# Attention of the first batch with transposes on PE and float32 products, and division behind the product

## The chip, the cores and the metric

The kernel runs on one core of a Trainium2 chip. The metric is device time in microseconds, the median of three runs. The core has a matmul engine (TensorE, PE below; its weight loads are PEld), a vector engine (VectorE, DVE), an activation engine (ScalarE, ACT), GpSimd (POOL) and SyncE (SP), which here only issues DMAs. PE writes its results to PSUM, which has eight banks of 512 float32 columns.

## What is computed

Three stages follow each other: attention with normalised q and k (4 batches, 12 heads, 448 positions, 64 columns), a gated layer with a matrix over the positions (`moe1` in the kernel), and a residual MLP behind a layer norm (`moe2`). All is float32.

```python
rms = lambda x, g: x / sqrt(mean(x * x, -1) + 1e-6) * g
s = (rms(q, g_q) @ rms(k, g_k).T) / sqrt(64)
p = exp(s - max(s)); p = p / (sum(p) + 1e-9)
x = heads_to_columns(p @ v)                     # 4 x 448 x 768
h = relu(x @ w_in); u, w = h[:512], h[512:]     # split of the 1024 columns
x = (u * (w_spatial @ norm(w) + b_spatial)) @ w_out
out = x + relu((norm(x) * g_ln) @ w_ch1) @ w_ch2
```

## The kernel before

**Numbers.** A float32 matrix is held as two float16 matrices, a high part and what is left (hi and lo), and a product is three float16 matmul passes (hi hi, hi lo, lo hi). Much of the work on DVE and ACT makes these parts. ACT makes hi by a converting copy, DVE makes lo as `x * scale - hi`, in one instruction.

**Attention.** It goes by pairs of heads; pair `i` of 24 belongs to batch `i // 6`. `att_load` (L156) loads q, k and v of a pair: q with its positions laid out `(n p)`, in rows of 256 bytes, k as `(p n)`, v twice, once for each half of the partitions. `att_front` and `att_back` (L171, L191) normalise q and k, split them, and turn them with a DMA transpose into `hT`. `att_v` (L208) scales v on POOL (L214), splits it on ACT and POOL (L215, L216). `s_mm` (L223) makes the scores of a group of two blocks of 128 rows; block 3 lies across both heads and runs as two 64-row halves (L232), the others as whole matmuls (L236). `softmax1` (L240) takes the maximum (L246, L247) and the exponentials with their sums (L251). `softmax2` (L260) makes the scaled reciprocal of the sums (L265, L266), the high part of the probabilities (L271, ACT) and the low part (L274, DVE), into `p16`, and one DMA transpose per group turns `p16` into `pT` (L276). `av_mm` (L280) multiplies with v: eleven steps, for each head 384 columns and then 64 (L293), the two heads on the two halves of PE's columns, into the single bank `ps_o`. `av_out` (L297) splits the result into `xT` (L304, L305). `att_slot` (L313) puts these in program order; the product of pair `i - 1` stands in the slot of pair `i`.

**The stages.** Pairs 0 to 6 run beside `moe1_weights` (L430), which loads the weights as 64-bit floats, rebuilds float32 by integer operations on DVE (L386 to L388) and splits them. The pairs of the next batch run beside `moe1` of the batch before (L482). The last `moe1` runs beside the layer norms and the first products of `moe2` (L612), which then goes on alone to the end. PSUM before `moe2`: three banks `ps_m` for `moe1` and the small sums, one `ps_o`, two times two for the scores (`ps_s`).

**The order.** At the end `issue_order` (L875) replaces the program order of each engine by that of a list scheduler, `schedule` (L796). It uses the costs of `hold` (L702), in ns, for instance for DMAs:

```python
    if kind == "InstDmaTransposeAnt":
        return 490 + 0.83 * n, 1325, 0.875 * n
    if kind == "InstDMACopy":
        ...
        x = p * b / (180 if short else 360)
```

The last value is the time of the transfer itself. The priorities are disturbed and relaxed again as the list `SHAKES` (L666) says.

## Time and profile before

| | us |
|---|---|
| median of 3 runs (lowest, highest) | 1217.05 (1215.68, 1217.31) |
| the profiled execution | 1218.43 |
| its span, first to last instruction | 1216.6 |
| PE busy | 1053.8 (87%) |
| DVE busy | 925.8 (76%) |
| ACT busy | 594.5 (49%) |
| POOL busy | 246.6 (20%) |

Busy time is an average over stages that have different limits, so the stretches are read one by one: attention of the first batch with the moe1 weights (until about 190 us), attention of the other batches with moe1 (190 to 480), the last moe1 with the first of moe2 (480 to 570), moe2 (570 to the end). PE's busy time contains the modelled end of each matmul, so matmuls that stand apart look longer than they pace in a dense row. Several names of a tile are joined in a row (`pT<-p`), and a row's mean is that of one instruction.

### The profile page before, as it was taken

To read this page: it belongs to the slowest core of one execution; us is meant where nothing else is said; L and a number is where in the kernel's file an instruction comes from. 1 tells how busy PE (TensorE), PEld (TensorE's weight loads), DVE (VectorE), ACT (ScalarE), POOL (GpSimd) and SP (SyncE) were. 2 spreads that over 40 slices of the span, in tenths; PEclk is the share of its full clock that TensorE was granted. 3 is DMA by queue.
4 is the path that set the end of the run, shared out by engine and by line. 5 is a ranking of instruction groups with operands and counts; after the bars stand their busy time and mean duration, and the time that the engine had idled before them with its cause. 6 is when DMAs were issued, how large, how long until landed. Compare 5 with 4: busy or idle time off the path is not lost.

```text
span 1216.6 us, 17589 instructions
## 1 busy us (share of the span) xinstructions
PE 1053.8 (87%) x6444; PEld 552.3 (45%) x6444; DVE 925.8 (76%) x1992; ACT 594.5 (49%) x1122; POOL 246.6 (20%) x164
## 2 busy tenths in 40 slices
...
GB/s 192 257 221 252 213 206 198 193 192 208 203 200 203 186 180 153 244 163 210 246 117 27 27 79 104 1 105 38 68 34 71 79 26 104 1 52 1 1 52 130
DMA packets 289430, 159.28 MB, mean 131 GB/s; under 512 B 253568, under 2 KB 266944, under 8 KB 289344
## 3 DMA queue, kind: packets, MB, share of 16 engines
...
## 4 chain that ended last, share of the span: by engine, by line
PE 58%; DVE 22%; DMA 9%; issue 4%; ACT 3%; POOL 2%; SPq 1%; ACTq 0%; POOLq 0%; DVEq 0%
PE ps L627 27%; PE ps L646 26%; DVE p L274 6%; DVE nb L246 4%; DMA pT<-p 2%; DVE nb L247 1%; DMA xnT<-xn 1%; DVE raw L197 1%; POOL rs L184 1%; DMA vraw<-in_v_dram 1%; PE pso L564 1%; PE ps_s L236 1%; DVE sm L265 1%; PE psu L523 1%; PE ps_o L293 1%
## 5 line engine op out<-in xcount | busy, mean ns | idle before, releaser
L646 PE MATMUL ps<-xnT,wt 128*128 128x384 f16 (+1 forms) x1728 | 358.6, 354 | 5.7 <-DMA xnT<-xn 5.7
L627 PE MATMUL ps<-wt,h 128*128 128x384 f16 x2016 | 356.3, 326 | 0.0
L630 DVE SCALAR_TENSOR_TENSOR x<-ps,wio,x 128x384 f32<-128x384 f32 x336 | 198.8, 613 | 131.7 <-PE ps L627 130.9
L627 PEld LDWEIGHTS <-h 128*128 128x128 f16 x2016 | 196.6, 98 | 136.9 <-ACT h L650 0.7
L646 PEld LDWEIGHTS <-wt 128*128 128x128 f16 x1728 | 168.1, 98 | 157.0 <-DMA xnT<-xn 6.2
L649 ACT ACTIVATE hf<-ps 128x512 f32<-128x512 f32 (+1 forms) x96 | 51.2, 540 | 354.0 <-PE ps L646 345.3
L236 PE MATMUL ps_s<-hT 128*128 128x448 f16 x288 | 88.1, 417 | 112.6 <-ACT pexp L251 77.4
L274 DVE SCALAR_TENSOR_TENSOR p<-pexp,sm,p 128x448 f16<-128x448 f32 x168 | 133.4, 811 | 7.9 <-ACT p L271 7.8
L251 ACT ACTIVATE pexp<-ps_s,nb,cs 128x448 f32<-128x448 f32 x168 | 119.8, 716 | 32.9 <-DVE nb L247 16.7
L271 ACT ACTIVATE p<-pexp,sm 128x448 f16<-128x448 f32 x168 | 104.2, 660 | 23.6 <-DMA pT<-p 9.9
L293 PE MATMUL ps_o<-pT,v 128*64 128x64 f16 (+1 forms) x1056 | 87.3, 297 | 23.4 <-DVE xT L305 13.1
L651 DVE TENSOR_TENSOR h<-hf,h 128x512 f16<-128x512 f32 (+1 forms) x96 | 59.1, 619 | 62.4 <-ACT h L650 61.7
L236 PEld LDWEIGHTS <-hT 128*128 128x128 f16 x288 | 27.9, 105 | 157.8 <-issue 89.0
L246 DVE TENSOR_REDUCE nb<-ps_s 128x2 f32<-128x896 f32 x96 | 92.0, 960 | 4.0 <-PE ps_s L236 2.4
L293 PEld LDWEIGHTS <-v 128*64 128x64 f16 x1056 | 51.1, 122 | 67.4 <-issue 21.1
L502 PE MATMUL psv<-w_v,xT 128*128 128x512 f16 (+1 forms) x360 | 68.0, 346 | 4.8 <-DVE xT L305 2.6
L523 PE MATMUL psu<-xT,w_u 128*128 128x448 f16 x288 | 64.3, 359 | 0.0
L184 POOL TENSOR_TENSOR rs<-ss,mhalf 128x28 f32<-128x28 f32 (+1 forms) x12 | 57.9, 4827 | 26.9 <-DVE sm L265 9.7
L357 ACT ACTIVATE wt<-r_f 128x1536 bf16<-128x1536 f32 x24 | 35.4, 1475 | 50.9 <-PE ps L627 44.6
L200 POOL TENSOR_TENSOR qk<-raw,qk 128x896 f16<-128x896 f32 x23 | 47.9, 2084 | 53.6 <-ACT qk L199 45.7
L650 ACT ACTIVATE h<-hf 128x512 f16<-128x512 f32 (+1 forms) x96 | 54.5, 575 | 5.4 <-PE ps L627 3.0
L387 DVE SCALAR_TENSOR_TENSOR r_f<-r_w,r_f 128x256 int32<-128x256 int32 (+1 forms) x96 | 53.5, 560 | 1.1
...
## 6 DMA issues: line engine op xcount, KB each, us to landing
...
```

Source lines behind the costliest of these rows:

```text
L184: nc.gpsimd.tensor_tensor(rs, ss, c.mhalf[:, 0:14 * m], op=ALU.pow)
L236: nc.tensor.matmul(ps[:, :S], p.hT[:, blk, :], kt[:, :, hd * 64:hd * 64 + 64], start=(t == 0), stop=(t == 1))
L246: nc.vector.tensor_reduce(nb[:, 0:n], ps[:, 0:n, :S], axis=AX.X, op=ALU.max, negate=True)
L251: nc.scalar.activation(pe[:, j, :], ps[:, j, :S], AF.Exp, bias=nb[:, j:j + 1], scale=c.cs[:, 0:1], accum_out=sm[:, j:j + 1])
L271: nc.scalar.activation(hi, x, AF.Copy, scale=sm[:, j:j + 1])
L274: nc.vector.scalar_tensor_tensor(lo, x, sm[:, j:j + 1], hi, op0=ALU.mult, op1=ALU.subtract)
L293: nc.tensor.matmul(p.po[hd * 64:hd * 64 + 64, c0:c1], p.v16[:, hd, u], p.pT[:, blk:blk + nb, ch, r0:r1], start=(n == 0), stop=(n == len(mm ...
L502: nc.tensor.matmul(ps[m * h:m * h + m, 0:hn], xT[:, k, x, t * P:t * P + m], wv[:, w, k, h * hn:(h + 1) * hn], start=(n == 0), stop=(n == l ...
L523: nc.tensor.matmul(ps[:, :S], wu[:, w, k, f * P:(f + 1) * P], xT[:, k, x, :], start=(n == 0), stop=(n == len(mms) - 1))
L627: nc.tensor.matmul(ps[:, 0:384], h16[:, f, h, t * P:(t + 1) * P], w2[:, w, f, e * 384:(e + 1) * 384], start=(i == 0), stop=(i == len(mms) ...
L630: nc.vector.scalar_tensor_tensor(xs, ps[:, 0:384], io[:, 0:1], xs, op0=ALU.mult, op1=ALU.add)
L646: nc.tensor.matmul(ps[:, 0:nn], w1[:, w, d, f * P:(f + 1) * P], xnT[:, a:a + n, x * NC6 + d, :], start=(i == 0), stop=(i == len(mms) - 1))
```

## The change

For the pairs of the first batch (0 to 5, `PE_PAIRS`) the exponentials stay float32. PE transposes them against an identity matrix, 28 blocks of 128 x 128 per pair (the last of four column blocks overlaps the third), into PSUM (`ps_t`, two banks), ACT copies them to `pT`, and PE multiplies them with the unsplit v in float32, four column blocks for each of two heads. These pairs have no `att_v`, no `p16`, no low part, no DMA transpose of `p16`, and no third load of v.

For all pairs the probabilities are no longer divided by their sum before they are turned. A new `av_scale` makes the reciprocals of seven sums, spreads them as a diagonal (`dg`, DVE), turns them into a row for each head with one float32 matmul into `ps_o`, and ACT copies that row to `rb`. `av_out` multiplies the product by it (DVE) and splits. The later pairs keep the float16 parts of the exponentials, two blocks in one instruction and without a scale from a tile.

q is loaded as `(p n)` like k, in runs of 1792 bytes. With it every block of rows holds positions of both heads, so all score blocks run in two halves, and the product runs with all 448 columns at once. Several tiles change their place (`gk`, `vpre`, `sq` with two buffers, the position weights loaded in two parts). PSUM has `ps_x` with one bank for the sums, `ps_t` with two until pair 6 is done, then `ps_m` with two; `moe2` gets five banks `ps_f` instead of four. The order model takes other DMA times, a cost of float32 matmuls, and a port that some DVE and POOL instructions share; `SHAKES` is another list.

```diff
 def att_load(c, i):
-    nc.sync.dma_start(out=r[:, 0:NB, :], in_=c.q[b, h0:h0 + 2].rearrange("h s d -> (h s) d").rearrange("(n p) d -> p n d", p=P))
+    nc.sync.dma_start(out=r[:, 0:NB, :], in_=c.q[b, h0:h0 + 2].rearrange("h s d -> (h s) d").rearrange("(p n) d -> p n d", p=P))
...
-    nc.sync.dma_start(out=vr[64:128, :, 6, :], in_=vs[:, :, 0, :])
+    if i not in PE_PAIRS:
+        nc.sync.dma_start(out=vr[64:128, :, 6, :], in_=vs[:, :, 0, :])
...
 def att_v(c, i):
+    if i in PE_PAIRS:
+        return
...
+CHUNKS = (0, 128, 256, S - 128)
+PE_PAIRS = {0, 1, 2, 3, 4, 5}
...
 def s_mm(c, i, g):
-            if blk == 3:
-                for hd in range(2):
...
-            else:
-                hd = int(blk > 3)
-                nc.tensor.matmul(ps[:, :S], p.hT[:, blk, :], kt[:, :, hd * 64:hd * 64 + 64],
-                                 start=(t == 0), stop=(t == 1))
+            for hd in range(2):
+                nc.tensor.matmul(ps[hd * 64:hd * 64 + 64, :S], p.hT[:, blk, hd * 64:hd * 64 + 64],
+                                 kt[:, :, hd * 64:hd * 64 + 64], start=(t == 0), stop=(t == 1))
...
 def softmax2(c, i, g):
-    nc.vector.tensor_scalar(sm[:, 0:n], sm[:, 0:n], 1e-9, 2.0 ** -14, op0=ALU.add, op1=ALU.mult)
-    nc.vector.reciprocal(sm[:, 0:n], sm[:, 0:n])
...
-            nc.scalar.activation(hi, x, AF.Copy, scale=sm[:, j:j + 1])
...
-        nc.vector.scalar_tensor_tensor(lo, x, sm[:, j:j + 1], hi, op0=ALU.mult, op1=ALU.subtract)
+    if i in PE_PAIRS:
+        for j, blk in enumerate(GROUPS[g]):
+            pt = c.ps_t.tile([P, 512], F32, tag="ps_t", name=f"ps_t{i}_{blk}")
+            for ch, k0 in enumerate(CHUNKS):
+                nc.tensor.transpose(pt[:, ch * P:(ch + 1) * P], p.pe[g][:, j, k0:k0 + P], c.ident[:])
+            nc.scalar.activation(p.pT[:, blk * 512:(blk + 1) * 512], pt, AF.Copy)
+        return
+    x = p.pe[g][:, 0:n]
+    p16 = c.att.tile([P, 2, 2, S], F16, tag="p16", name=f"p16_{i}_{g}", bufs=3)
+    nc.scalar.activation(p16[:, 0:n, 0], x, AF.Copy, scale=2.0 ** 14)
+    nc.vector.scalar_tensor_tensor(p16[:, 0:n, 1], x, 2.0 ** 14, p16[:, 0:n, 0], op0=ALU.mult, op1=ALU.subtract)
...
 def av_mm(c, i):
+    if i in PE_PAIRS:
+        pT = p.pT.rearrange("p (b c q) -> p b c q", b=NB, c=4)
+        for ch in range(4):
+            p0 = 64 if ch == 3 else 0
+            for hd in range(2):
+                nc.tensor.matmul(p.po[hd * 64:hd * 64 + 64, :S], p.vr[p0:, hd, 5 if ch == 3 else 2 * ch],
+                                 pT[p0:, :, ch, hd * 64:hd * 64 + 64], start=(ch == 0), stop=(ch == 3))
+        return
...
+    for n, (ch, u) in enumerate(mms):
+        for hd in range(2):
+            nc.tensor.matmul(p.po[hd * 64:hd * 64 + 64, :S], p.v16[:, hd, u], pT[:, :, ch, hd * 64:hd * 64 + 64],
+                             start=(n == 0), stop=(n == len(mms) - 1))
+
+
+def av_scale(c, i):
...
+    nc.vector.tensor_scalar(p.sm, p.sm, 1e-9, None, op0=ALU.add)
+    nc.vector.reciprocal(p.sm, p.sm)
+    dg = c.att.tile([P, 64, NB], F32, tag="dg", name=f"dg{i}", bufs=1)
+    nc.vector.tensor_tensor(dg, p.sm[:].unsqueeze(1).to_broadcast([P, 64, NB]),
+                            c.eye2[:].unsqueeze(2).to_broadcast([P, 64, NB]), op=ALU.mult)
+    pr = c.ps_o.tile([P, 512], F32, tag="ps_o", name=f"ps_r{i}")
+    nc.tensor.matmul(pr[:, :S], c.head, dg.rearrange("p q n -> p (q n)"), start=True, stop=True)
+    p.rb = c.att.tile([P, S], F32, tag="dg", name=f"rb{i}", bufs=1)
+    nc.scalar.activation(p.rb, pr[:, :S], AF.Copy, scale=2.0 ** 14 if i in PE_PAIRS else 1.0)
...
 def av_out(c, i):
-    nc.scalar.activation(xT[:, hp, 0, :], p.po[:, :S], AF.Copy, scale=2.0 ** -14)
-    nc.vector.scalar_tensor_tensor(xT[:, hp, 1, :], p.po[:, :S], 2.0 ** -14, xT[:, hp, 0, :], op0=ALU.mult, op1=ALU.subtract)
+    x = c.att.tile([P, S], F32, tag="xo", name=f"xo{i}", bufs=1)
+    nc.vector.tensor_tensor(x.rearrange("d (p n) -> d p n", n=NB), p.po[:, :S].rearrange("d (n p) -> d p n", n=NB),
+                            p.rb.rearrange("d (p n) -> d p n", n=NB), op=ALU.mult)
+    if i in PE_PAIRS:
+        split(c, x, xT[:, hp, 0, :], xT[:, hp, 1, :], c.sv[b][:, 0:1])
+    else:
+        nc.scalar.activation(xT[:, hp, 0, :], x, AF.Copy)
+        nc.vector.tensor_tensor(xT[:, hp, 1, :], x, xT[:, hp, 0, :], op=ALU.subtract)
...
 def hold(i, eng, kind):
-        return 490 + 0.83 * n, 1325, 0.875 * n
+        return 490 + 0.83 * n, 1325, 1.17 * n
...
-        x = p * b / (180 if short else 360)
+        x = p * b / (218 if short else 256)
...
     if eng == "PE":
+        if any(x.dtype == F32 for x in i.ins):
+            return n * 4 / 2.37 + 2 if n > P else 115, 0, 0
...
 def tile_attention_moe_moe2_kernel(...):
-    c.ps_m = c.ps_x = ps_m = pool("ps_m", "left", 3, space=PSUM)
+    c.ps_x = pool("ps_x", "left", 1, space=PSUM)
+    c.ps_t = pool("ps_t", "left", 2, space=PSUM)
...
+    c.ident = eye = c.wraw.tile([P, P], F32, tag="ident", name="ident", bufs=1)
+    make_identity(nc, eye[:])
+    c.eye2 = c.const.tile([P, 64], F32, name="eye2")
+    nc.vector.tensor_tensor(c.eye2, eye[:, 0:64], eye[:, 64:P], op=ALU.add)
+    c.head = c.const.tile([P, P], F32, name="head")
...
+    c.ps_t.release()
+    c.ps_m = ps_m = pool("ps_m", "left", 2, space=PSUM)
...
-    c.ps_f = pool("ps_f", "right", 4, space=PSUM)
+    c.ps_f = pool("ps_f", "right", 5, space=PSUM)
```

## Rows read from the trace of the kernel before

**Rows 1.** Stretches: length, busy us per engine (instructions), granted clock, DMA share, GB/s.

```profile
core 0: us, PE busy (x) PEld busy (x) DVE busy (x) ACT busy (x) POOL busy (x), PEclk, DMA share, GB/s
0.00:30.00 30.00, 0.93 (x2) 0.13 (x2) 12.24 (x35) 5.31 (x6) 4.64 (x8) 1.00 0.89 191
30.00:190.00 160.00, 73.64 (x432) 30.68 (x432) 155.54 (x299) 121.52 (x240) 79.42 (x40) 0.85 1.02 228
190.00:360.00 170.00, 147.72 (x1073) 69.89 (x1071) 165.50 (x347) 143.80 (x295) 95.49 (x58) 0.96 1.04 199
360.00:480.00 120.00, 106.77 (x755) 50.85 (x757) 105.90 (x230) 92.04 (x188) 47.84 (x36) 0.93 0.92 181
...
570.00:1217.00 647.00, 641.58 (x3694) 359.94 (x3694) 413.23 (x891) 180.47 (x320) 0.00 (x0) 1.00 0.20 66
...
120.00:150.00 30.00, 14.23 (x76) 6.05 (x77) 30.00 (x63) 21.79 (x45) 13.42 (x8) 0.61 0.99 220
```

**Rows 2.** Chain of waits, shares by line, 30 to 190 us and 190 to 480.

```profile
by line: DVE p L274 15.0%; DVE nb L246 13.0%; issue 9.0%; DMA u_w<-in_moe_w_in_dram 5.4%; DVE raw L197 4.8%; DMA pT<-p 3.6%; DMA o_w<-in_moe_w_out_dram 3.4%; DVE nb L247 3.2%; DVE u_f L388 3.2%; POOL rs L184 3.0%; DVE o_f L387 2.9%; DVE sm 
...
by line: DVE p L274 15.6%; DVE nb L246 10.6%; issue 10.3%; DMA pT<-p 5.0%; PE psu L523 4.5%; PE ps_s L236 4.3%; DVE nb L247 4.1%; PE ps_o L293 3.9%; POOL rs L184 3.4%; DVE sm L265 3.1%; ACT pexp L251 2.9%; DVE raw L197 2.8%; ACT p L271 2.2%
```

**Rows 3.** Groups by line and form: DVE and POOL in attention and moe1.

```profile
L274 DVE SCALAR_TENSOR_TENSOR p<-pexp,sm,p 128x448 f16<-128x448 f32 x168 | 133.4, 811 | 7.9 <-ACT p L271 7.8
...
L265 DVE TENSOR_SCALAR sm<-sm 128x2 f32<-128x2 f32 x72 | 23.2, 325 | 1.1 <-ACT pexp L251 0.9
...
L265 DVE TENSOR_SCALAR sm<-sm 128x1 f32<-128x1 f32 x24 | 3.4, 140 | 0.0
...
L266 DVE RECIPROCAL sm<-sm 128x2 f32<-128x2 f32 x72 | 10.8, 152 | 0.2
...
L305 DVE SCALAR_TENSOR_TENSOR xT<-ps_o,xT 128x448 f16<-128x448 f32 x24 | 14.6, 609 | 3.1 <-ACT xT L304 3.1
...
L551 DVE SCALAR_TENSOR_TENSOR g<-u,wsc_g,g 128x448 f16<-128x448 f32 x16 | 9.9, 675 | 0.9 <-ACT g L550 0.9
...
L200 DVE TENSOR_TENSOR qk<-raw,qk 128x896 f16<-128x896 f32 x1 | 1.1, 1082 | 0.0
...
L216 POOL TENSOR_TENSOR v<-vraw,v 128x512 f16<-128x512 f32 x24 | 31.8, 1327 | 5.0 <-ACT v L215 5.0
```

**Rows 4.** Instructions on the tile sm: count, duration min/median/max ns, first and last start.

```profile
L274 DVE SCALAR_TENSOR_TENSOR p<-pexp,sm,p x168: 658/672/2309, 45.5 to 471.6; 128x448 f16<-128x448 f32 x168
```

**Rows 5.** Groups by line and form: ACT copies and conversions.

```profile
L271 ACT ACTIVATE p<-pexp,sm 128x448 f16<-128x448 f32 x168 | 104.2, 660 | 23.6 <-DMA pT<-p 9.9 <-DVE sm L266 7.0 <-issue 2.3
...
L199 ACT ACTIVATE qk<-raw 128x896 f16<-128x896 f32 x24 | 22.6, 943 | 17.1 <-DVE raw L197 13.9 <-DMA hT<-qk 3.2
...
L649 ACT ACTIVATE hf<-ps 128x512 f32<-128x512 f32 x48 | 28.0, 590 | 121.1 <-PE ps L646 116.2 <-DVE r_f L387 3.3 <-PE pssc L83 1.6
...
L550 ACT ACTIVATE g<-u,wsc_g 128x448 f16<-128x448 f32 x16 | 9.4, 655 | 4.7 <-DVE wsc_g L90 4.4 <-DVE wsc_g L89 0.3
```

**Rows 6.** Instructions on the tile pT: the transposes on SP's queue.

```profile
L276 SPq DMA_TRANSPOSE pT<-p x96: 1221/1645/4265, 46.8 to 472.3; - x96
```

**Rows 7.** Groups by line and form: PE and its weight loads.

```profile
L236 PE MATMUL ps_s<-hT 128*128 128x448 f16 x288 | 88.1, 417 | 112.6 <-ACT pexp L251 77.4 <-DMA hT<-qk 24.9 <-DMA hT<-hT 7.1
...
L293 PE MATMUL ps_o<-pT,v 128*64 128x384 f16 x528 | 74.9, 390 | 23.4 <-DVE xT L305 13.1 <-DMA pT<-p 6.1 <-POOL v L216 2.3
...
L523 PE MATMUL psu<-xT,w_u 128*128 128x448 f16 x288 | 64.3, 359 | 0.0
...
L236 PEld LDWEIGHTS <-hT 128*128 128x128 f16 x288 | 27.9, 105 | 157.8 <-issue 89.0 <-DMA hT<-qk 34.2 <-DMA hT<-hT 13.4
...
L293 PE MATMUL ps_o<-pT,v 128*64 128x64 f16 x528 | 19.5, 205 | 0.0
...
L232 PE MATMUL ps_s<-hT 128*64 128x448 f16 x96 | 17.5, 444 | 0.0
...
L83 PE MATMUL pssc<-ssb,ones 128*128 128x1 bf16 x24 | 4.0, 167 | 0.8 <-DVE ssb L80 0.8
```

99 lines of the change are left out of this document (52 added, 47 removed).

## The prediction

> **What bounds the kernel now.** First the stretches [rows 1]. From 570 us on PE is busy 641.6 of 647 us at full clock: moe2 is a wall of matmuls, which the change leaves as it is, apart from which PSUM pool its banks come from. Whatever can be won lies before. Between 30 and 190 us (attention of the first batch beside the conversion of the moe1 weights) DVE is busy 155.5 of 160 us and the DMA engines have work throughout (share 1.02), while PE has 73.6 us and ACT 121.5. Between 190 and 480 us (attention of the other batches beside moe1) DVE has 165.5 + 105.9 = 271.4 of 290 us, PE 147.7 + 106.8 = 254.5, ACT 235.8, DMA about full. So the first stretch is held by DVE and DMA with PE idle half the time; in the second, DVE and PE are close to each other. The chains of waits say the same [rows 2]: L274, the low half of the probabilities, is the largest piece of both, then L246; no PE line is named in the first stretch, and PE lines come in with 4 to 5% each in the second.
>
> **What each pair costs now and after, on DVE.** Removed per pair [rows 3]: seven L274 at 811 ns (5.68 us), L265 three times at 325 and once at 140 (1.12), four L266 at 152 (0.61), L305 (0.61): 8.01 us. Added for every pair by the division behind the product: an add over 7 columns (0.14 to 0.33, taken 0.25), a reciprocal (0.15), the diagonal `dg` with 448 columns (L551's form at 675, or L274's at 811: 0.74), the product out of PSUM (L305's 0.61), the low part (0.74 again): 2.49 us. A pair of the first batch has no low half of the exponentials left, so it saves 8.01 - 2.49 = 5.5 us, six pairs 33. A later pair keeps them, without a scale operand, three times with 896 columns (L200 on DVE has 1082 ns; stretched as L274 is, 1310; taken 1.2) and once with 448 (0.74): 4.34, so it saves 1.2 us, 18 pairs 21. The stretching is worth a look [rows 4]: L274 takes 672 ns at the median but up to 2309, so 168 x 139 ns = 23 us of its time is something holding it. First-batch pairs also lose L216 on POOL (1.3 us) and L214. If POOL is what holds DVE, up to 126 x 0.139 = 17 us more could go in the later pairs; I count none of it, and some in the low end.
>
> The Trainium skill (SBUF — State Buffer, on its shared port pair) says that a DVE instruction with two SBUF inputs contends with a GpSimd instruction that reads SBUF. The spread from 658 to 2309 ns agrees, and by that rule `dg` and the new low part are open to it too, which the 0.74 already covers.
>
> **ACT.** [rows 5] First batch, per pair: seven L271 (4.62), L215 (the form of L199: 0.94) and L304 go; seven copies of 512 columns out of PSUM (L649, 0.59 each: 4.13), the copy `rb` (the form of L304, which it replaces) and the high part with a scale (L550: 0.66) come. That is 0.8 us less, six pairs 5. Later pairs get three copies of 896 (0.94) and one of 448 (0.66) for seven of 0.66, `rb` for L304, and the high part: 0.5 us less. The new copies stand between two PE steps, which L271 did not.
>
> **DMA.** A first-batch pair drops the transposes of p16, 7 x 2 x 448 x 128 x 2 bytes = 1.6 MB; at the stretch's 228 GB/s [rows 1] that is 7.0 us, six pairs 42 of the 163 us (1.02 x 160) of work. Its third load of v (32 KB) goes too. In the queue they leave SP free: one L276 transpose holds SP's queue 1.6 us at the median and up to 4.3 [rows 6], and the loads of q, k, v and weights stand behind it. The load of q in contiguous runs of 1792 bytes, not 256, costs no more than before; its gain lies between 0 and its whole transfer (224 KB, 1.0 us a pair), counted 0.
>
> **PE, where the trace shows least.** No row has a float32 matmul or a transpose on PE, so both are bounded [rows 7]. A dense pass of 448 columns paces at 64.3 / 288 = 223 ns (L523), so 128 columns stream in 64 ns; a weight load takes 105 ns (L236) and overlaps PE.
> - 28 transposes per pair: low, stream alone, 28 x 64 ns = 1.8 us; high, four passes each with its load in the open, 28 x 4 x 169 ns = 18.9. Taken: the load sets the pace as loads overlap in every PE row here, 28 x 0.105 = 2.9.
> - Eight float32 products of 448 columns: low, one pass with the two halves of PE side by side as L293 runs now (four pairs of 0.33: 1.3 us); high, four passes each with a 105 ns load in the open, 8 x 4 x 328 = 10.5. Taken: four passes one behind the other, 8 x 4 x 223 = 7.1, since the new `hold` books four times the columns and no discount for the second half.
> - L293 in float16 goes: (74.9 + 19.5) / 24 = 3.9 us. The product for `rb` comes: 4 x 223 = 0.9 (0.2 to 1.3).
> - Scores in halves: twelve L236 at 306 (88.1 / 288) and two L232 pairs at 365 become 14 pairs: 0.7 more, 0.1 if the longer time of those rows is only waiting.
> Sum: 2.9 + 7.1 - 3.9 + 0.9 + 0.7 = 7.7 us per pair (-0.5 to 27.5), six pairs 46. Later pairs: +0.9 +0.7, and L293 in one form of 448 columns (eleven steps in 24 pairs: 94.4 us / 264 = 358 ns; its part of 384 columns alone, 284, stretched to 448, 331) -0.3: 1.3 us, 0.7 with scores at 0.1; 17 pairs behind 190 us make 22, or 12.
>
> The Trainium skill (FP8 and Floating Point Precision, TensorE Precision Notes) gives true FP32 four passes through the array. No run here shows it; by it the product would be the 7.1 taken, or 3.6 if the halves still run side by side, which would take PE to 99 us and leave the forecast where it is.
>
> **The sum.** First stretch: DVE 155.5 - 33 = 122, PE 73.6 + 46 = 120, DMA 163 - 42 = 121, ACT 121.5 - 5 = 117. Four engines equally full cannot each run at the 97% that DVE reaches alone: in 360 to 480 us, where three share the load, the fullest stands at 89%. I take 92%: 122 / 0.92 = 133 for 160, a gain of 27 (ends: 97%, 126, gain 34; 80%, 152, gain 8). Second stretch: DVE 271.4 - 20 = 251, PE 254.5 + 12 to 22 = 267 to 277. PE becomes the fuller one. The fullest stood at 93.6%; 271 (near the lower end, as the longer L232 holds waits) / 0.936 = 289 for 290, a gain of 1 (ends 267 / 0.97 = 275, gain 15; 277 / 0.92 = 301, loss 11). Start: identity, `eye2` and `head` are built beside the first loads, where DVE is busy 12.2 of 30 us [rows 1]; 1 us lost (0 to 4, the whole if POOL's first work waits for it). moe2 gets two banks for its first products and five for its second, in place of three and four: PE is idle 5.4 us there in all, counted 0, loss below that as much again. `ps_x`, single, serves only the few sums. The new order follows other DMA times and a port that DVE and POOL share: 10 us either way from the waits on DMA at L236 and L293, counted 0. In all -27 - 1 + 1 = -27. The profiled execution took 1218.4 us (span 1216.6), so 1191; it lies 1.4 above the median of 1217.05, so 1190.
>
> **The rivals.**
> - *Transposes in the open* (time 1209, against the median): each pays its load and the full length of a short matmul, which L83 shows with 167 ns [rows 7]. 28 x (0.10 + 0.167) = 7.5 us instead of 2.9, PE 73.6 + 74 = 147, at 97% 152 of 160; the 1 us lost at the start comes back later: gain 8. For: each has new weights or new data of 128 columns only. Against: L232's and L293's short loads overlap. The Trainium skill (TensorE: Matmul & The Clock Gate, Part 4) puts a transpose in a kernel at about 275 ns, which would be 7.7 us. No run here shows it.
> - *A round trip takes the place of the wait removed* (time 1219): ps_o is one bank, and each pair now uses it twice, for `rb` and for the product. Add, reciprocal, `dg`, product, copy: 0.25 + 0.15 + 0.74 + 0.9 + 0.59 = 2.6 us; half of it uncovered in 24 pairs is 31 us, and the 27 are gone, a loss of 4 at most. It decides from 1.1 us per pair. For: L293 waited 23.4 us in 24 pairs already, most for DVE's L305 [rows 7]. Against: moe1's matmuls and the next scores can lie between, and the sums are there before the product is needed.
> - *Slower: PE becomes the bound of the first batch* (time 1279). It decides from (0.97 x 160 - 73.6) / 6 = 13.6 us added per pair. With transposes at 18.9 us a pair adds 23.7, PE has 216 us, at 97% 222 for 160: 62 lost, the rest even: 1217 + 62. For: nothing in the trace excludes it. Against: 13.6 needs both float32 costs near their high ends.
> - *Low clock* (time 1281). From 120 to 150 us the granted clock was 0.61, mostly the lower of its two levels (1.2 and 2.4 GHz), with PE busy 14.2 of 30 us [rows 1]. If it stays low in the whole stretch, 73.6 x 0.85 + 46 = 109 us at full clock become 217, at 97% 224 for 160: 64 lost. Against: PE gets fuller, and fuller stretches here stand at 0.93 and above. The same Part 4 of that page says that transposes do not count as busy, which would speak for it; by it the 2.9 us per pair do not help the clock, but the products still do.
> - *More gain* (1160): DVE keeps 97% and the stretching goes.
>
> **How the numbers follow.** Forecast 0.60, more gain 0.08, transposes in the open 0.10, round trip 0.08, PE bound 0.09, low clock 0.05. The range 1158 to 1224: low, gains of 34 and 15 and 10 from order and stretching, 1 lost; high, 8 won, 11 and 4 lost. The two rivals near 1280 stay outside. 0.2% (2.4 us) is about what a measurement of this kernel can tell from no change: faster 0.77, same 0.08, slower 0.15.
>
> **What would show it.** Right: in the stretch up to moe1's first matmuls DVE's busy time some 33 us less, no `pT` transposes for six pairs, that stretch near 135 us; `rb` chains without idle PE before the products. Wrong: transposes or float32 products well over 0.105 and 0.9 us each on PE; PE idle before the products until ACT or DVE; a granted clock near 0.6 in the first batch; or the second stretch longer than 290 us.

## The result and the profile after

| | before | after |
|---|---|---|
| median, us (lowest to highest, 4 runs each) | 1216.37 (1214.41 to 1217.31) | 1205.26 (1202.38 to 1207.18) |
| profiled execution, its span | 1218.4, 1216.6 | 1205.7, 1203.9 |

The ratio is 0.9909 (95% interval 0.9884 to 0.9933): the change gains 11 us where 27 were forecast. The sign and the place were right and the size was less than half of it; 1205 lies inside the range.

Busy time of the engines over the whole span, from the page of after:

```profile
PE 1088.6 (90%) x6385; PEld 569.8 (47%) x6385; DVE 884.5 (73%) x1804; ACT 580.9 (48%) x1088; POOL 232.5 (19%) x154
```

DVE has 41 us less than before (925.8), PE 35 more (1053.8), as meant. So the question is why 41 us less on the engine that held the first batch gave 12.7 us of span (the first to the last instruction of the profiled execution). Below, the *first batch* ends with DVE's last write of xT for its six pairs, the *later batches* with that of all 24 pairs; what follows is moe1 of the last batch and moe2, "the rest". Stretches of before, cut there (columns as in [rows 1]), and then the same of after with the first 30 us in front:

```profile
30.00:192.80 162.80, 73.88 (x432) 30.68 (x432) 158.34 (x304) 123.77 (x243) 81.17 (x42) 0.85 1.02 227
192.80:482.60 289.80, 256.84 (x1859) 122.36 (x1860) 269.23 (x574) 234.27 (x480) 141.58 (x93) 0.95 0.98 190
482.60:1216.60 734.00, 722.18 (x4153) 399.13 (x4151) 485.99 (x1083) 231.15 (x395) 19.25 (x22) 0.99 0.27 84
```

```profile
0.00:30.00 30.00, 0.96 (x4) 0.31 (x5) 17.95 (x49) 7.41 (x9) 9.24 (x11) 1.00 0.84 214
30.00:175.20 145.20, 103.57 (x527) 47.02 (x527) 125.60 (x231) 118.54 (x247) 58.88 (x29) 0.84 0.75 188
175.20:465.20 290.00, 263.67 (x1705) 122.56 (x1705) 254.05 (x443) 223.35 (x439) 147.24 (x92) 0.95 0.93 185
465.20:1203.90 738.70, 720.36 (x4151) 399.89 (x4149) 486.94 (x1084) 231.62 (x395) 17.19 (x22) 0.99 0.28 84
```

The first batch ends 17.6 us earlier, the later batches take 290.0 us against 289.8, the rest takes 738.7 against 734.0. In the first batch DVE falls from 158.3 busy us to 125.6 (33 were forecast), ACT from 123.8 to 118.5, the DMA share from 1.02 to 0.75, and PE rises from 73.9 to 103.6. But DVE, busy for 97% of the stretch before, is busy for 125.6 / 145.2 = 86.5% after, and the others for less: nobody is full any more. In the later batches PE passes DVE (263.7 against 254.1), and the length stays.

The new work on PE, ACT and DVE, by form, in the first batch and then in the later ones:

```profile
L271 PE MATMUL ps_t<-ident,pexp 128*128 128x128 f32 x168 | 31.2, 320 | 16.6 <-ACT pexp L257 13.4 <-ACT pT L272 3.0
L251 DVE TENSOR_REDUCE nb<-ps_s 128x2 f32<-128x896 f32 x25 | 27.0, 1084 | 7.1 <-PE ps_s L240 6.6 <-ACT pexp L257 0.4
L272 ACT ACTIVATE pT<-ps_t 128x512 f32<-128x512 f32 x42 | 24.6, 618 | 5.0 <-PE ps_t L271 4.9
...
L294 PE MATMUL ps_o<-pT,vraw 128*64 128x448 f32 x72 | 20.0, 619 | 3.0 <-ACT rb L317 3.0
...
L315 PE MATMUL ps_r<-dg,head 128*128 128x448 f32 x14 | 9.5, 772 | 1.5 <-DVE dg L312 1.5
...
L294 PE MATMUL ps_o<-pT,vraw 64*64 64x448 f32 x24 | 7.8, 606 | 0.0
...
L312 DVE TENSOR_TENSOR dg<-sm,eye 128x448 f32<-128x448 f32 x7 | 5.1, 722 | 0.0
L251 DVE TENSOR_REDUCE nb<-ps_s 128x1 f32<-128x448 f32 x8 | 5.0, 619 | 1.3 <-PE ps_s L240 1.3
...
L315 PEld LDWEIGHTS ps_r<-dg,head 128*128 128x128 f32 x14 | 2.7, 240 | 4.4 <-DVE dg L312 1.6 <-PE ps_s L240 1.5 <-DVE nb L252 0.7
```

```profile
L277 DVE SCALAR_TENSOR_TENSOR p<-pexp,p 128x896 f16<-128x896 f32 x48 | 58.4, 1216 | 5.1 <-ACT p L276 5.0
...
L301 PE MATMUL ps_o<-pT,v 128*64 128x448 f16 x396 | 45.9, 362 | 2.1 <-ACT rb L317 2.1
...
L315 PE MATMUL ps_r<-dg,head 128*128 128x448 f32 x34 | 18.1, 616 | 2.9 <-DVE dg L312 1.9 <-DVE sst_g L85 0.9
```

The chain of waits of the first batch has changed its head: ACT's exponentials (12.2%) and the scores on PE (6.9%) stand ahead, with a load of raw behind them (6.8%), where the low half of the probabilities and the maxima led before [rows 2].

```profile
by line: ACT pexp L257 12.2%; issue 10.2%; PE ps_s L240 6.9%; DMA raw<-in_k_dram 6.8%; ACT sq L181 4.9%; DVE raw L200 4.9%; DVE nb L251 4.3%; POOL rs L187 3.9%; ACT pT L272 3.6%; PE ps_t L271 3.6%; DMA pT<-p 3.4%; ACT vpre L139 3.3%; DMA v_
```

Two holes are worth seeing. The first is in the first batch at 90 to 107 us, where every engine is idle for a third to a half of the time (busy: PE 9.4, DVE 11.6, ACT 8.1, POOL 8.9 of 17 us). On POOL, then on SP's queue:

```profile
82.54 1.90 POOL L203 TENSOR_TENSOR qk<-raw,qk 128x896 f16<-128x896 f32 x1 [2.16 <-ACT qk L202]
90.47 0.71 POOL L147 PARTITION_ALL_REDUCE vam<-vmx  x1 [6.04 <-DVE w_u L393]
98.82 1.88 POOL L203 TENSOR_TENSOR qk<-raw,qk 128x896 f16<-128x896 f32 x1 [7.64 <-issue]
100.67 5.56 POOL L187 TENSOR_TENSOR rs<-ss,mhalf 128x28 f32<-128x28 f32 x1
```

```profile
100.73 0.34 SPq L162 DMA_DIRECT2D raw<-in_q_dram  x1
101.11 0.43 SPq L163 DMA_DIRECT2D raw<-in_k_dram  x1
```

POOL's all-reduce, for the v scale of the next batch, is recorded with 0.71 us, but the next instruction of POOL starts 7.64 us later, with no releaser ("issue"); the data of that one, ACT's L202, were there at 92.2. It is L203, which releases the buffer for the next raw, whose load goes out at 100.73; ACT's square of that raw waits for it at 104.69 and stands ahead of the next exponentials. None had run since 86.8 us. In front of the all-reduce POOL is idle too, from 84.44 to 90.47, although the input `vmx` was there at 83.67; the L393 that its row names does not write it.

```profile
83.52 0.15 DVE L144 TENSOR_REDUCE vmx<-vparts 128x1 f32<-128x3 f32 x1
```

The kernel before has the same all-reduce in its first batch. These are its POOL, and then the stretches between the two neighbours of the all-reduce, before and after:

```profile
49.05 2.35 POOL L200 TENSOR_TENSOR qk<-raw,qk 128x896 f16<-128x896 f32 x1 [5.06 <-ACT qk L199]
57.25 0.38 POOL L146 PARTITION_ALL_REDUCE vam<-vmx  x1 [5.86 <-DVE p L274]
64.58 4.84 POOL L184 TENSOR_TENSOR rs<-ss,mhalf 128x28 f32<-128x28 f32 x1 [6.96 <-DVE ssb_v L80]
```

```profile
51.40:64.58 13.18, 4.73 (x18) 1.46 (x17) 12.19 (x35) 7.95 (x18) 0.38 (x1) 1.00 1.08 239
...
84.44:98.82 14.38, 6.66 (x31) 2.41 (x31) 11.67 (x27) 10.27 (x20) 0.71 (x1) 0.67 0.79 194
```

So POOL stood still nearly as long before the change, but DVE had other work: it was idle for 1.0 us beside that hold. Beside the one of after it was idle for 2.7 us, and for another 3.0 behind it (102.7 to 105.7).

The second is in the rest. Waits of PE from the end of the attention to 640 us, before and after:

```profile
PE ps L646 <- DMA xnT<-xn: 5.7, 1, 5.7
```

```profile
PE ps L681 <- DMA xnT<-xn: 11.0, 2, 10.3
```

and SP's queue ahead of the long one in after:

```profile
528.04 7.87 SPq L641 DMA_TRANSPOSE xnT<-xn  x2
535.97 2.32 SPq L628 DMA_DIRECT2D lx<-x2d  x2
...
548.18 8.53 SPq L641 DMA_TRANSPOSE xnT<-xn  x3
```

Two transposes of xnT hold SP's queue for 7.9 us; the two loads of lx behind them, whose data were wanted for the next layer norm, go out at 535.97, and moe2's matmuls L681 wait for 10.3 us, where those of before waited for 5.7. This is read from the trace; no run moves the two transposes.

### The profile page after: what moved, and what is told of

Same layout as the page of the kernel before. It is cut to its first block, busy times and chain, and to the rows that moved or that the text cites. A ratio compares the mean times of both kernels' runs of the same rounds, so it can differ in the third digit from the quotient of the medians.

```text
span 1203.9 us, 17146 instructions
## 1 busy us (share of the span) xinstructions
PE 1088.6 (90%) x6385; PEld 569.8 (47%) x6385; DVE 884.5 (73%) x1804; ACT 580.9 (48%) x1088; POOL 232.5 (19%) x154
## 4 chain that ended last, share of the span: by engine, by line
PE 71%; DVE 8%; DMA 8%; ACT 8%; issue 4%; POOL 1%; SPq 1%; ACTq 0%; DVEq 0%; POOLq 0%
PE ps L662 27%; PE ps L681 27%; PE ps_s L240 3%; ACT pexp L257 3%; PE pso L599 3%; PE psu L558 3%; PE pss L571 2%; PE ps_o L301 2%; PE psv L537 2%; DMA raw<-in_k_dram 2%; DMA hT<-qk 1%; DVE nb L251 1%; DVE p L277 1%; PE ps_r L315 1%; DVE raw L200 1%
## 5 line engine op out<-in xcount | busy, mean ns | idle before, releaser
L681 PE MATMUL ps<-xnT,wt 128*128 128x384 f16 (+1 forms) x1728 | 348.6, 354 | 11.0 <-DMA xnT<-xn 11.0
L662 PE MATMUL ps<-wt,h 128*128 128x384 f16 x2016 | 346.3, 326 | 0.0
L681 PEld LDWEIGHTS <-wt 128*128 128x128 f16 x1728 | 168.3, 98 | 164.0 <-DMA xnT<-xn 10.8
L240 PE MATMUL ps_s<-hT 128*64 128x448 f16 x672 | 100.3, 401 | 63.3 <-ACT pexp L257 27.2
L240 PEld LDWEIGHTS <-hT 128*64 128x64 f16 x672 | 39.5, 117 | 116.8 <-issue 69.4
L277 DVE SCALAR_TENSOR_TENSOR p<-pexp,p 128x896 f16<-128x896 f32 x72 | 77.9, 1082 | 10.0 <-ACT p L276 9.8
L276 ACT ACTIVATE p<-pexp 128x896 f16<-128x896 f32 x72 | 61.6, 860 | 3.6 <-DMA pT<-p 3.5
L558 PE MATMUL psu<-xT,w_u 128*128 128x448 f16 x288 | 59.5, 355 | 3.0 <-ACT u L561 1.5
L537 PE MATMUL psv<-w_v,xT 128*128 128x512 f16 (+1 forms) x360 | 61.8, 343 | 0.0
L203 POOL TENSOR_TENSOR qk<-raw,qk 128x896 f16<-128x896 f32 x23 | 45.8, 1990 | 65.4 <-ACT qk L202 33.7
L417 DVE SCALAR_TENSOR_TENSOR r_f<-r_w,r_f 128x256 int32<-128x256 int32 (+1 forms) x96 | 53.1, 554 | 1.4
L418 DVE SCALAR_TENSOR_TENSOR r_f<-r_w,r_f 128x256 int32<-128x256 int32 (+1 forms) x96 | 53.0, 553 | 1.2
L599 PE MATMUL pso<-w_o,g 128*128 128x384 f16 x288 | 52.6, 336 | 0.5 <-ACT x2o L602 0.3
```

Of the source, the lines that this page charges most:

```text
L240: nc.tensor.matmul(ps[hd * 64:hd * 64 + 64, :S], p.hT[:, blk, hd * 64:hd * 64 + 64], kt[:, :, hd * 64:hd * 64 + 64], start=(t == 0), stop= ...
L276: nc.scalar.activation(p16[:, 0:n, 0], x, AF.Copy, scale=2.0 ** 14)
L277: nc.vector.scalar_tensor_tensor(p16[:, 0:n, 1], x, 2.0 ** 14, p16[:, 0:n, 0], op0=ALU.mult, op1=ALU.subtract)
L537: nc.tensor.matmul(ps[m * h:m * h + m, 0:hn], xT[:, k, x, t * P:t * P + m], wv[:, w, k, h * hn:(h + 1) * hn], start=(n == 0), stop=(n == l ...
L558: nc.tensor.matmul(ps[:, :S], wu[:, w, k, f * P:(f + 1) * P], xT[:, k, x, :], start=(n == 0), stop=(n == len(mms) - 1))
L599: nc.tensor.matmul(ps[:, 0:384], g16[:, f, g, s0:s0 + m], wo[:, w, f, e * 384:(e + 1) * 384], start=(n == 0), stop=(n == len(mms) - 1))
```

## Experiments

Stages of each kernel's profiled execution, us, cut as above:

| kernel | first batch ends | later batches | rest | span |
|---|---|---|---|---|
| before | 192.8 | 289.8 | 734.0 | 1216.6 |
| after | 175.2 | 290.0 | 738.7 | 1203.9 |
| e1 no float32 way | 210.6 | 312.6 | 732.7 | 1255.9 |
| e2 after, one list | 172.2 | 313.3 | 738.2 | 1223.7 |
| e3 before, one list | 187.4 | 308.2 | 736.5 | 1232.1 |
| e4 product twice | 186.2 | 309.5 | 736.1 | 1231.8 |
| e5 short all-reduce | 169.0 | 290.1 | 738.6 | 1197.7 |
| e6 transposes twice | 183.1 | 290.9 | 738.6 | 1212.6 |
| e7 pT copies twice | 193.1 | 291.2 | 739.2 | 1223.5 |
| e8 maxima twice | 195.2 | 292.1 | 739.8 | 1227.1 |
| e9 no float32 way, own list | 192.9 | 324.1 | 731.2 | 1248.2 |
| e10 before, new model | 207.5 | 313.0 | 734.2 | 1254.7 |
| e11 after, old model | 155.7 | 312.1 | 737.5 | 1205.3 |
| e12 after, other list | 175.3 | 296.4 | 735.3 | 1207.0 |
| e13 no float32 way, old model | 187.7 | 306.5 | 736.3 | 1230.5 |
| e14 later rb products twice | 174.5 | 297.3 | 738.2 | 1210.0 |
| e15 later diagonals twice | 177.9 | 296.0 | 740.4 | 1214.3 |
| e16 scale on PE, long list | 182.9 | 288.1 | 739.9 | 1210.9 |
| e17 scale on PE, old model | 157.3 | 299.3 | 738.0 | 1194.6 |
| e18 scale on PE, mixed model | 160.5 | 290.2 | 733.7 | 1184.4 |

Ratios below are to the kernel before on the same chip; after has 0.9909.

### First round: parts undone, one list

**e1_no_pe_pairs.**
```
-PE_PAIRS = {0, 1, 2, 3, 4, 5}
+PE_PAIRS = set()
```


> The changed kernel with no pair on the float32 way: the first batch too goes through float16 parts and DMA transposes; division behind the product, the layout of q, the PSUM pools and the order model stay. Theory: the gain comes from the first batch alone (its end came 17.6 us earlier, the later batches took 290.0 us after 289.8), so this gives 1213 to 1220, that is 8 to 15 over the changed kernel. Rival: the division behind the product and q's layout carry part of the gain: below 1212. Rival: they cost time that the float32 way pays for: over 1221.

1259.4 us, ratio 1.0355 (1.0329 to 1.0382).

**e2_after_one_list** and **e3_before_one_list**: the list of shakes cut to its first entry.
```
-SHAKES = ((0, 0, 4), (1003, 1000, 3), (1005, 8000, 4), ...
+SHAKES = ((0, 0, 4),)
```


> The changed kernel with its order from the list scheduler without the disturbances (only the first entry of the list of shakes). Theory: the gain lies in the work that left DVE and DMA, so beside the kernel before treated the same way it still wins 8 to 20 us; by itself it is 0 to 15 us slower than the changed kernel, 1205 to 1220. Rival (the gain is the order's): it is no faster than the kernel before treated the same.

> The kernel before with its order from the list scheduler without the disturbances. Theory: 0 to 15 us slower than the kernel before, 1217 to 1232, and 8 to 20 us slower than the changed kernel treated the same. Rival (the gain is the order's): the two treated alike differ by less than 4 us.

After 1228.4 us, ratio 1.0108 (1.0069 to 1.0148); before 1231.9, 1.0124 (1.0096 to 1.0153). Treated alike, the two kernels are not told apart: 2 us by the ratios, 3.4 by the medians. This is what the rival in both expectations named (the gain is the order's), and not the 8 to 20 us of the theory.

**e4_product_twice.**
```
-        for ch in range(4):
+        for ch in (0, 1, 2, 3, 0, 1, 2, 3):
```


> The changed kernel with each float32 product with v made twice, the second overwriting the first (same output): 28 us more on PE in the first batch by the 27.8 us that those 48 products take now. Theory (PE is not what paces the first batch, it is idle 41 of 145 us there): 0 to 7 us more, 1205 to 1212. Rival (the float32 work on PE paces it): 14 to 28 more, 1219 to 1233.

1231.7 us, ratio 1.0121 (1.0093 to 1.015).

What follows from the four: the order is a quantity of its own. Whatever redraws it without a search lengthens the later batches from 290 to 308 to 313 us, in both kernels and in stretches that the edit doesn't touch. The tuned list is worth 15 us to before and 24 to after. So e1 and e4 price their edit and a new order together and can't be read alone: of e4's 26 us over after 19.5 lie in the later batches, where no product was doubled, and 11.0 in the first. From here on, edits either keep after's order, instruction by instruction (the planner books the unedited program, and a doubled instruction is put right behind its twin), or get a search of their own.

### Second round: one cause at a time, after's order kept

**e5_short_all_reduce.**
```
-        nc.gpsimd.partition_all_reduce(am[:], mx[:], channels=P, reduce_op=bass_isa.ReduceOp.max)
+        nc.gpsimd.tensor_copy(am[:], mx[:])
...
+        if "vam" in out.bass_ap.tensor.name and getattr(i, "op", None) != ALU.pow:
+            return 8000, 0, 0
```


> The kernel after in its own order of instructions (the planner still books the old cost), with POOL's all-reduce of the v maxima of batches 1 to 3 replaced by a copy, so that each partition keeps its own scale for these batches: the maximum over the partitions is left out. Theory 1, POOL holds the hole at 90 to 107 us (all-reduce, then the q/k product, then the load of the next raw, then ACT's square ahead of the exponentials): that hole closes, the last xT of the first batch is written 6 to 10 us earlier than the 175.2 us of after, and some 1197 us in all. Theory 2, the hole belongs to the copies of hT behind bulk loads on DMA: the milestone moves by 2 us at most and the time stays at 1203 to 1206.

The second part of the edit lets the planner book the copy with the 8000 ns that it books for the all-reduce.

1201.0 us, ratio 0.9845 (0.9807 to 0.9883). The first batch ends at 169.0, 6.2 us earlier, and everything behind keeps that lead. POOL and the stretch of the hole (after had 9.36 us on PE, 11.62 on DVE, 8.11 on ACT and 8.89 on POOL there):

```profile
80.76 1.89 POOL L203 TENSOR_TENSOR qk<-raw,qk 128x896 f16<-128x896 f32 x1 [2.01 <-ACT qk L202]
82.60 0.64 POOL L147 COPY vam<-vmx 128x1 f32<-128x1 f32 x1
90.46 1.88 POOL L203 TENSOR_TENSOR qk<-raw,qk 128x896 f16<-128x896 f32 x1 [7.21 <-ACT qk L202]
92.30 5.25 POOL L187 TENSOR_TENSOR rs<-ss,mhalf 128x28 f32<-128x28 f32 x1
```

```profile
90.00:107.00 17.00, 12.42 (x58) 4.96 (x59) 15.59 (x25) 12.08 (x25) 12.36 (x7) 0.70 0.94 217
```

L203 now runs at 90.46 and not at 98.82, the load of raw goes out at 92.36, and DVE fills 15.6 of the 17 us. Theory 1 holds: POOL, an engine at 19% of the span, made the hole. But of the 6.2 us 1.8 are there before the copy (the first L203 starts at 80.76, in after at 82.54), a difference between two executions, so the hold is worth 4.4 us by these two traces; by the ratios the whole edit is worth 7.8, with an interval of several us.

**e6_transposes_twice, e7_pT_copies_twice, e8_maxima_twice.** Each wraps one line in a helper that issues it a second time for the six pairs:
```
-    nc.tensor.transpose(pt[:, ch * P:(ch + 1) * P], p.pe[g][:, j, k0:k0 + P], c.ident[:])
+    twice(nc, lambda: nc.tensor.transpose(pt[:, ch * P:(ch + 1) * P], p.pe[g][:, j, k0:k0 + P], c.ident[:]), i)
...
-    nc.scalar.activation(p.pT[:, blk * 512:(blk + 1) * 512], pt, AF.Copy)
+    twice(nc, lambda: nc.scalar.activation(p.pT[:, blk * 512:(blk + 1) * 512], pt, AF.Copy), i)
...
-    nc.vector.tensor_reduce(nb[:, 0:n], ps[:, 0:n, :S], axis=AX.X, op=ALU.max, negate=True)
+    twice(nc, lambda: nc.vector.tensor_reduce(nb[:, 0:n], ps[:, 0:n, :S], axis=AX.X, op=ALU.max, negate=True), i)
```


> The kernel after in its own order; each of the 168 float32 transposes of the first batch is made a second time right behind the first: about 31 us more on PE (168 x 186 ns), nothing else moves. Forecast's theory, four engines equally full so that none has slack: at least half of it shows, 16 to 31 us, all before the last xT of batch 0. Rival, the first batch is held by ACT and DVE in turn and PE has slack (103.6 of 145 us busy): under 10 us.

> The kernel after in its own order; each of ACT's 42 copies of the transposed exponentials out of PSUM is made twice in a row: 42 x 618 ns = 26 us more on ACT in the first batch. Forecast's theory (equal fill): 13 to 26 us. Rival, ACT is the one that holds (it had no gap at 60 to 90 and 127 to 150 us): all of it, 24 to 30 us, the most of the three doublings. Rival, DVE holds: under 13 us.

> The kernel after in its own order; each of DVE's 24 maxima of the first batch's scores is taken twice in a row: 18 x 1084 + 6 x 619 ns = 23 us more on DVE. Forecast's theory (DVE still the fullest at 125.6 of 145 us, others near it): 15 to 23 us. Rival, ACT holds and DVE only follows: under 12 us.

Ratios 0.9949 (0.993 to 0.9969), 1.0045 (1.0026 to 1.0064) and 1.0046 (1.0026 to 1.0067): 4.9, 16.5 and 16.7 us over after. The doubled groups in the first batch of each (line numbers are shifted by the helper):

```profile
L285 PE MATMUL ps_t<-ident,pexp 128*128 128x128 f32 x336 | 48.8, 296 | 15.6 <-ACT pexp L271 14.0 <-ACT pT L286 1.4
```

```profile
L286 ACT ACTIVATE pT<-ps_t 128x512 f32<-128x512 f32 x84 | 48.8, 596 | 4.2 <-PE ps_t L285 2.8
```

```profile
L265 DVE TENSOR_REDUCE nb<-ps_s 128x2 f32<-128x896 f32 x43 | 46.7, 1087 | 8.2 <-PE ps_s L254 7.5
...
L265 DVE TENSOR_REDUCE nb<-ps_s 128x1 f32<-128x448 f32 x14 | 8.6, 618 | 0.2
```

Against the rows of after, PE got 48.8 - 31.2 = 17.6 us more, ACT 48.8 - 24.6 = 24.2, DVE 55.3 - 32.0 = 23.3. The first batch grew by 7.9, 17.9 and 20.0 us, so a microsecond costs 0.45 us on PE, 0.74 on ACT and 0.86 on DVE by the traces, and 0.28, 0.68 and 0.72 by the ratios of the whole. ACT and DVE are not told apart; both stay in the range that the forecast's theory gave. PE, under 10 us, is not the fourth equal engine: there its rival is met. Each trace is one execution, and the end of the first batch moves by 1 to 3 us where next to nothing in it was edited (e14, e15 below). No engine is free, and the three prices add up to 1.7 to 2. That would fit a stage that is a chain from one engine to the next (score, maximum, exponential, transpose, copy, product) as much as a load on one of them: a doubled instruction adds its time to both. That such a chain is what left the fullest engine at 86.5% is argued from these prices and not shown by them.

### Third round: the order model

**e9_no_pe_pairs_own_list**: e1's edit, and
```
+SHAKES = ((0, 0, 6), (1002, 3000, 2))
```


> The kernel after without the float32 way (PE_PAIRS empty: all 24 pairs go through p16 and DMA transposes, with the division behind the product), with shakes searched by the order model for this program (140 tries, the best by the model kept). Theory 1, the float32 way is where the gain comes from and the other parts (division behind, q in runs, PSUM split, order model) bring nothing or cost: 1222 to 1250 us. Theory 2, the 1259 us of the same program under after's shakes was a bad order, and the division behind, which takes 24 x 1.2 = 29 us off DVE, gains by itself: 1200 to 1215 us.

1250.6 us, ratio 1.0241 (1.0192 to 1.0289).

**e10_before_new_model**: in before,
```
-        return 490 + 0.83 * n, 1325, 0.875 * n
+        return 490 + 0.83 * n, 1325, 1.17 * n
...
-        x = p * b / (180 if short else 360)
+        x = p * b / (218 if short else 256)
...
+        o.port = takes_port(i, o.eng, kind)
```


> The kernel before, its instructions as they are, ordered by after's order model (DMA times 1.17 and 218/256, the port of DVE and POOL, the register chain) with shakes searched for it by the model (140 tries). Forecast: the model by itself is worth 0, at most 10 us either way: 1207 to 1227 us. Rival, the model is where the measured gain comes from: 1200 to 1207 us. Rival, one list is as good as another only for its own model, and the order gets worse: over 1227 us.

1254.9 us, ratio 1.0279 (1.0235 to 1.0323).

**e11_after_old_model**: the same in after, the other way round, with `o.port = False`.

> The kernel after, its instructions as they are, ordered with before's DMA times (0.875, 180/360) and without the port, with shakes searched for it (140 tries). If the model counts for nothing (forecast): 1200 to 1210 us, as after. If it counts for as much as the whole measured gain: 1215 us and more.

1205.9 us, ratio 0.9876 (0.9829 to 0.9923).

**e12_after_other_list**:
```
+SHAKES = ((0, 0, 6), (1000, 1000, 3), (1001, 8000, 3), (1002, 3000, 2), (1004, 8000, 4))
```


> The kernel after with another list of shakes, found in the same number of tries, that the order model rates the same as after's own (its end 1167.7 against 1168.3 us). It tells how far two orders that the model calls equal lie apart on the chip. If the model's end is a good measure: 1201 to 1210 us. If luck of the order counts for as much as the change: outside 1195 to 1216 us.

1213.4 us, ratio 0.9958 (0.9933 to 0.9983).

**e13_no_pe_pairs_old_model**: e1's edit with the model of e11.

> The kernel after without the float32 way, ordered with before's DMA times and without the port, shakes searched for it (140 tries). All other parts of the change are in it, so it answers to the kernel before (1217 to 1219 us, its own model) on one side and to the run of after under the old model (1205.9 us) on the other. Theory 1, the float32 way is the whole gain: 1217 us or more. Theory 2, the division behind gains by itself what it takes off DVE (24 x 1.2 = 29 us at 0.5 us each): 1200 to 1210 us. If it stays at 1250 us as under the new model: the other parts cost 30 us, and the model is not to blame.

1233.2 us, ratio 1.011 (1.0082 to 1.0137).

Ratios to before, side by side:

| program | before's DMA times | after's model |
|---|---|---|
| before | 1 | 1.0279 |
| after without the float32 way | 1.0110 | 1.0241 |
| after | 0.9876 | 0.9909; other list 0.9958 |

Down each column: the float32 way is worth 1.0110 - 0.9876 = 2.3% under the one model and 2.8 to 3.3% under the other, 28 to 40 us; the other parts bring nothing that shows (1.1% lost or 0.4% won, with orders in between). Each entry has a list of its own, and before under its own DMA times has the list that it came with, so differences of half a per cent between entries say nothing. The whole change under one model is worth 1.2% on the left, 3.7% on the right, and 0.2% where each kernel has one list (e2, e3): its gain depends on the order that goes with it. Across: the new model brings nothing to after, and costs 34 us (before) and 16 us (without the float32 way) where all pairs still go through DMA transposes. So theory 1 of e9 and e13 holds (e9 at the upper end of its range), and of e1's 54 us over after, by these lists, 40 are the float32 way and 14 a bad order. e10 is what its second rival named: the order gets worse.

Two orders that the model rates alike (e12) lie 0.5% apart, about 6 us, between what its two theories gave. That is half of the change's own gain, and it bounds what any pair of kernels with redrawn orders can tell.

e11 shows more: its first batch ends at 155.7 us, 37 us before that of the kernel before, and its later batches take 312.1 us. The whole is as after's. An order can move time between the stages. It can also change how full the fullest engine is. Here are the first batches of e3 and e10, the program of before, and of e11, the program of after:

```profile
30.00:187.40 157.40, 70.95 (x420) 28.59 (x419) 149.82 (x303) 118.06 (x231) 77.92 (x40) 0.84 1.01 226
...
30.00:207.50 177.50, 71.49 (x414) 30.34 (x414) 155.49 (x317) 120.62 (x239) 76.10 (x40) 0.70 0.91 204
...
30.00:155.70 125.70, 98.62 (x514) 45.64 (x515) 109.27 (x214) 107.70 (x225) 39.92 (x20) 0.92 0.73 186
```

DVE fills 95% and 88% of its first batch in the one program, which had 97% in its own order, and 87% in the other, as in after: e11 is shorter there because 16 us of DVE's work stand behind it, not because DVE is fuller. In the eight kernels with the float32 way and no doubled instruction DVE stands between 83% (e2, e12) and 91% (e17).

### Fourth round: the later batches, and a better kernel

**e14_later_rb_products_twice** and **e15_later_diagonals_twice**: after's order, the helper put around L315 and around L312, for the 18 later pairs.

> The kernel after in its own order; the product that spreads the reciprocals (L315) is made twice in a row in the 18 later pairs: 18 x 1.15 = 21 us more on PE between the last xT of the first batch and that of the last. Forecast's step (PE becomes the fuller engine there): at least 12 us slower. Rival, DVE still holds and PE has slack: under 8 us.

> The kernel after in its own order; the diagonal of reciprocals (L312) is made twice in a row in the 18 later pairs: 18 x 0.69 = 12 us more on DVE in the same stretch. Forecast's step (PE is the fuller engine there): under 5 us slower. Rival, DVE still holds: 8 to 12 us.

Ratios 0.993 (0.9903 to 0.9956) and 0.9954 (0.9933 to 0.9975): 2.6 and 5.5 us over after. The doubled groups, in each kernel between 176 and 470 us:

```profile
L329 PE MATMUL ps_r<-dg,head 128*128 128x448 f32 x68 | 32.4, 602 | 2.9 <-DVE dg L326 1.9 <-DVE sst_g L85 0.9
```

```profile
L326 DVE TENSOR_TENSOR dg<-sm,eye 128x448 f32<-128x448 f32 x34 | 26.2, 770 | 0.7
```

PE got 32.4 - 18.1 = 14.3 us more and the later batches 297.3 - 290.0 = 7.3; DVE got 14.7 more (after has 11.5) and the batches 6.0. About half each by the traces, and less for PE by the ratios. e14 stays under 8 us, as its rival said (PE has slack), though not for nothing; e15, with 5.5 to 6 us, lies between the under 5 of the one expectation and the 8 to 12 of the other. So the forecast's step is not borne out: PE is the fuller engine by its busy time, but it does not hold the later batches alone.

**e16_scale_sum_on_pe_long_list**: the v scale of every batch is made as that of batch 0, by a sum on PE.
```
-    if b:
-        am = c.small.tile([P, 1], F32, tag="vam", name=f"vam{b}")
-        nc.gpsimd.partition_all_reduce(am[:], mx[:], channels=P, reduce_op=bass_isa.ReduceOp.max)
...
-    else:
+    if b == 0:
         nc.vector.tensor_tensor(mx, mx, mx, op=ALU.mult)
-        c.sv[b] = sum_scale(c, mx, f"V{b}", pool=c.const)
+    c.sv[b] = sum_scale(c, mx, f"V{b}", pool=c.const)
```


> A complete kernel: after with the v scales of batches 1 to 3 made as batch 0's is (sums of squares by a product on PE) in place of POOL's all-reduce, and a list of shakes searched longer (8000 tries, model's end 1157.7 against 1168.3 us). If the hole at 90 to 107 us comes out as gain, as with the short all-reduce: 1188 to 1200 us. If the new list gives it back elsewhere, as the other list of equal rating did: 1200 to 1215 us.

1204.4 us, ratio 0.9885 (0.9856 to 0.9914). Not told apart from after: the first batch ends at 182.9, later than after's 175.2, so the new order took back what the missing all-reduce could give.

**e17_scale_on_pe_old_model** and **e18_scale_on_pe_mixed_model**: e16's edit. e17 has the model of e11; e18 has this alone, and a list of 21 shakes:
```
-        x = p * b / (218 if short else 256)
+        x = p * b / (180 if short else 360)
```


> A complete kernel: after with the v scales of batches 1 to 3 made on PE in place of POOL's all-reduce, before's DMA times in the order model and no port, shakes searched in 5000 tries. If the gain of the first batch under these times (20 us against after) and the all-reduce's 6 us stay: 1185 to 1197 us. If the later batches take it back, as they did with after's program under these times: 1198 to 1212 us.

> The same complete kernel, with before's times for copies and after's time for transposes and its port, shakes searched in 6000 tries. If the too short time booked for transposes is what lengthened the later batches: these take 290 to 300 us and the whole 1187 to 1199 us. If order luck decides: 1200 to 1215 us, and no pattern in the stages.

1195.2 us, ratio 0.9803 (0.977 to 0.9836), and 1185.1 us, ratio 0.9722 (0.9689 to 0.9755). Stretches of e18, cut as above:

```profile
30.00:160.50 130.50, 97.89 (x521) 45.95 (x521) 117.36 (x229) 113.01 (x236) 58.85 (x28) 0.91 0.82 206
160.50:450.70 290.20, 269.76 (x1737) 127.68 (x1738) 259.69 (x451) 228.61 (x453) 148.25 (x88) 0.96 0.97 187
450.70:1184.40 733.70, 719.41 (x4128) 397.30 (x4126) 485.25 (x1084) 231.75 (x393) 19.91 (x22) 1.00 0.28 84
```

DVE fills 117.4 / 130.5 = 90% of the first batch, the later batches are back at 290, the rest at 733.7. Of the 14.7 us by which this first batch is shorter than after's, 8.2 are work that DVE does outside it. e18 beats both kernels, and its time lies 2 us below the range expected. Against e17 the longer booked time of the transposes and the port go with later batches that are 9 us shorter, as expected, but the lists differ too, and e12's 6 us are part of any such difference. The kernel before was not run with this model or so long a search, so e18's 33 us are not what the change alone is worth.

## Why the prediction was right and wrong

- *DVE, a pair of the first batch 5.5 us less, six 33*: met, 158.3 to 125.6 us, and in part by luck. In the first 30 us DVE is busy for 18.0 us where it was for 12.2, since three more pieces of `w_v` are converted there; from the start to the end of the first batch its busy time falls by 27.0. The terms were added up from the durations of single instructions, and in the trace these overlap: before, DVE's 1992 records last about 1048 us together and keep it busy for 925.8, 0.06 us less for each. The change takes 11 of 16 such instructions from each of the six pairs, 4 us in all. In the whole kernel the lines replaced fall from 189.0 to 134.3 us, 55 for the 54 booked, and DVE's busy time by 41.
- *ACT, 5 less*: right, 123.8 to 118.5.
- *DMA, 42 of 163 us less*: share 1.02 of 162.8 us, 166, to 0.75 of 145.2, 109: 57 less. The bound that this set, 121, was not needed.
- *PE, 7.7 us a pair (-0.5 to 27.5)*: near in sum at about 6.8, from parts that missed on both sides. Transposes 31.2 / 6 = 5.2 us a pair for 2.9; float32 products (20.0 us, and 7.8 in the form of the half with 64 rows) 27.8 / 6 = 4.6 for 7.1; `rb` 1.15 for 0.9; the scores 4.2 for 4.4, where 0.7 more were booked. The stretch as a whole has only 29.7 us more on PE, for 46, because 9.6 us of moe1's first products, which ran inside it before, now run behind it:

```profile
L502 PE MATMUL psv<-w_v,xT 128*128 128x512 f16 x32 | 9.6, 439 | 0.8 <-ACT xT L304 0.7
```

  In the later pairs PE gained where 1.3 us were booked as a loss: L301 takes 45.9 / 18 = 2.55 us a pair, and L293 took 3.7 there (3.9 over all pairs). The doubled transposes of e6 add 17.6 us / 168 = 105 ns each, the pace that was taken from the weight loads; in place they take 186, presumably because the exponentials arrive one by one. The length of one is something else:

```profile
L271 PE MATMUL ps_t<-ident,pexp x168: 272/273/476, 38.7 to 147.7; 128*128 128x128 f32 x168
```

  The Trainium skill (TensorE: Matmul & The Clock Gate, Part 4) gives about 275 ns for a 128 x 128 bf16 transpose in a kernel; the 273 ns of one float32 transpose here agree, but they overlap, so 28 of them cost 5.2 us and not the 7.7 that the prediction worked out from that figure. The Trainium skill's rule of four passes for true FP32 (FP8 and Floating Point Precision, TensorE Precision Notes) gave 7.1, or 3.6 with the halves side by side; the measured 4.6 lies between. With the whole array in use, the doubled `rb` product of e14 adds 14.3 us / 17 = 0.84 us, near four passes of 223 ns (0.89).
- *The first stretch: fullest engine at 92%, a gain of 27 (34 to 8)*: **the step that failed**, by its size. 86.5% gives 145 us for 163, a gain of 17.6, inside its ends. The fill was read from a stretch in which PE and DVE have separate work to choose from, moe1 beside attention. e5 shows the largest single piece of the missing 9.4 us: POOL's all-reduce, worth 4.4 to 6.2 us of them, which the sum did not name because POOL was half idle, though `hold` books 8000 ns for it in both kernels. Before, DVE was idle for only 1.0 us beside the same hold, since it had other work. What makes the rest stays open. The pairs that run through DVE, ACT and PE in turn are one account, for which the prices of e6 to e8 speak. The order is the other: no order tried of the float32 program stands above 91%, but the program of before falls from 97% to 88% under another list and model, so a fill belongs to an order as much as to a program.
- *The second stretch, 289 us for 290*: right as a length, 290.0, by luck. PE has 263.7 us where 267 to 277 were booked, and stands at 91%, not 93.6%; the two misses cancel. PE is the fuller engine there, as forecast, but from moe1's products that came over from the first batch, and it is not the one that decides (e14, e15).
- *The start, 1 us lost*: can't be seen apart, since the stages are cut behind it.
- *moe2, counted 0, up to 5.4 lost*: 4.7 were lost. The term named the banks; e1 and e18, with after's banks, have 732.7 and 733.7 us there, no more than before's 734.0. What the trace shows in their place is two transposes ahead of two loads in SP's queue; no run changes that alone.
- *The order model, 0, 10 either way*: 0 for after's program (e11), and 34 us lost on before's (e10). The order that a list gives moves a kernel by 6 to 24 us, which the ends covered for the first and not for the second.
- The rivals. *Transposes in the open*: its 1209 us is nearest to the 1205 measured, but by luck: a transpose lasts 273 ns, near the 267 taken, yet 28 cost 5.2 us of the 7.5, and PE has 103.6 us, not 147, and costs least. *Round trip through ps_o*: refuted; in all of the first batch L294 waits 3.0 us for ACT's `rb`, in the later ones L301 waits 2.1, far from the 1.1 us a pair that would decide. *PE becomes the bound*: refuted: PE has 30 us more, not the 142 of that sum. *Low clock*: refuted, 0.84 against 0.85, and 0.89 with twice as many transposes in e6. *More gain*: not in after; e18 has 33 us.

The sum of after: -17.6 in the first batch, 0, +4.7 in the rest: -12.7 of span. The forecast's 1190 is a time that nearly the same work on every engine can reach, since e18 takes 1185; what stands between e18 and after is the hold on POOL and another order, which e18 does not separate.
